# Sparse attention feeding a gated MLP: k, q and x turned by large DMA transposes, batch 1 turned by TensorE, rows loaded ahead, a new order of work

## The chip, the cores and the metric

The kernel runs on one core of one Trainium2 chip. The metric is the device time of one execution in microseconds (us). The profile is one further execution, taken by the hardware profiler; its times are counted from the start of its span. A run of the kernel before takes 227.52 us (median of 3, 227.52 to 228.05).

## What is computed

There are 4 batches of 8 heads, 768 positions and 64 numbers per head. Each query sees its own neighbourhood (fewer than 16 positions away) and 24 block keys, the maxima of k over blocks of 32 positions; the block values are the means of v. The attention output of all heads, 3072 rows of 512 numbers, then goes through an MLP with 2048 hidden units.

```python
k_sum = k.reshape(B, H, nb, block, D).max(axis=3)
v_sum = v.reshape(B, H, nb, block, D).mean(axis=3)
scores_l = scale * np.matmul(q, k.transpose(0, 1, 3, 2))
...
scores_s = scores_s + np.log(block)
scores_l_m = np.where(mask_l, scores_l, -1000000000.0)
scores_all = np.concatenate([scores_l_m, scores_s], axis=-1)
...
a = a / (np.sum(a, axis=-1, keepdims=True) + 1e-09)
v_all = np.concatenate([v, v_sum], axis=2)
return np.matmul(a, v_all).astype(np.float32)
```

```python
h = x @ w_in
relu6 = np.clip(h + 3.0, 0.0, 6.0)
g = h * relu6 / 6.0
return (g @ w_out).astype(np.float32)
```

## The kernel before

All matmuls are bf16. The attention of a batch works on four pairs of heads. The queries are cut into 12 blocks of 64, each with a window of 96 keys, and 24 block keys stand behind them, so that one score matmul has 120 rows of keys. For that, k and q must lie turned: the 64 numbers of a head on the partitions, the positions along the row. ScalarE takes the exponential out of PSUM (line 566), VectorE multiplies with the band mask (line 570), and TensorE multiplies with the values (line 671), which carry a column of ones so that the sum comes with them. VectorE divides (lines 705 and 709), TensorE turns the result (line 724), and a copy puts it into `x` (the helper in line 463).

The MLP works on eight tiles of 384 rows, two for each batch, numbered s = 0 to 7. One first-layer step has four matmuls of 384 columns (line 742), a ScalarE relu (line 747) and a VectorE multiplication (line 749), and there are 16 such steps for a tile. The second layer has 12 groups of four matmuls of 512 columns for a tile (line 762), a copy out and a store that SyncE (SP) issues (line 774).

Batch 0 has its own beginning: k and q are loaded in runs of rows and turned by TensorE (lines 479 and 522), half of the queries first, so that the MLP can begin early. Batches 1 to 3 load k and q in a raw form of 32 partitions (line 403: each load has 3072 pieces of 32 numbers), VectorE turns them in blocks of 32 x 32 (lines 623 and 627), and small copies by ScalarE or VectorE fill the overlap of the key windows. The means of v come from a matmul (lines 588 and 605). For batch 1 the values' overlap is copied on the chip; for batches 2 and 3 SP moves the overlap (lines 437 and 439) and the means (line 578) by DMA from SBUF to SBUF. Loads that change f32 to bf16 are issued by GpSimd (POOL), one after the other, through one queue.

Nothing is scheduled by hand within the loops: every operation is recorded with a name, and the string `ORDER` lists all names. `F21.3` is the fourth operation of the first layer of tile 2, in the second quarter of its hidden units; `G02` is the second layer of tile 0, rows 2; `s`, `v`, `u`, `h`, `w` are scores, values, means, overlap of v, and turning of k and q; `K`, `Q`, `V`, `I`, `O` are loads of k, q, v, w_in and w_out. A letter behind a colon chooses ScalarE or VectorE. `Plan.run` walks through the list, gives out buffers and PSUM banks, and sorts by its planned begin. Each engine then executes its own operations strictly in that order, so that a late operation holds up everything behind it on its engine. Of the 8 PSUM banks, 3 are for the first layer (`h`), 1 for the second (`o`), and 2 pairs for attention (`S`). Matmuls on a constant tile (`idle`, line 848) fill TensorE's planned gaps in the first 22 us.

Of the kernel before, what the change touches and what calls it, by code (L numbers as in the profile page):

```python
# [29 lines left out]
e.1 c.0 K00.0 c.8 z3.0 z1.0 z2.0 K01.0 c.1 Q000.0 K02.0 k00.0 c.2 Q010.0 c.3 c.4 e.0 k00.1 e.3 k00.2:D k00.4 V00.0 V01.0  # L30
k01.0 k01.2:A Q01w2.0 c.6 V02.0 V03.0 q010.0 q000.0 k01.1 k01.4 z0.0 q000.1:A q010.1:A k00.3:A Q01w1.0 I0.0 Q01w0.0 k01.3:A
k03.0 s000.0 k02.0 q030.0 k03.2:A q030.1:D e.2 c.7 I1.0 O0.0 I2.0 q020.0 s010.0 s000.1 s010.1 u00.0 q020.1:A s010.2 k03.1
k02.1 k03.4 k02.4 u00.1:A u00.2:D h010.0:D s000.2 u01.0 s030.0 s030.1 h011.0:D u01.1:D h000.0:D u01.2:D k02.2:A s020.0
s020.1 u02.0 h030.0:D u02.1:D s030.2 h020.0:A s020.2 u03.0 u03.1:D v01.0 v00.0 v00.2 v00.3 v01.2 v01.3 v02.1 I3.0 O2.0 O1.0
v00.1 v01.1 v02.4 v00.4 v00.5 h031.0:A h001.0:A k03.3:A u02.2:A v02.0 v00.6 v00.7:A v01.4 v02.2 v02.3 v01.5 q011.0 v01.6
v02.5 k02.3:A v01.7:D F00.0 v02.6 F00.5 F00.6 q001.0 v02.7:A F00.1 F00.2 q001.1:A F00.3 F00.7 c.5 h021.0:D q031.0 q011.1:A
F00.8 u01.3:D u00.3:D F00.4 F00.9 F01.0 q021.0 F01.3 F01.1 F01.2 q031.1:D F00.15 F00.10 s001.0 q021.1:A F01.4 F01.5 u03.2:D
F00.16 F00.17 s001.1 s001.2 s011.0 F00.11 F00.12 F00.13 F00.14 F01.9 F01.10 c.9 F01.11 F01.6 s011.1 F01.7 s011.2 F01.8
s021.0 F02.9 F02.10 F02.11 s021.1 s021.2 G02.0 s031.0 F02.0 F03.0 F03.3 s031.1 s031.2 F02.1 F03.1 F02.2 F03.2 v04.0 v03.0
v03.1 F03.4 v03.2 F03.5 v04.1 v04.2 F02.3 F02.6 F02.4 F02.5 v03.3 v03.4:A F03.9 v05.0 G02.1 v04.3 z0.1:P z3.1:P K11.0 K12.0  # L40
O3.0 K13.0 z1.1:P K10.0 V12.0 V10.0 V13.0 F03.10 F02.7 v05.1 v05.2 v05.3 v05.4:A F02.8 v04.4:D F03.11 F03.6 F03.7 F10.0
F03.8 F10.3 F10.1 F10.6 F10.4 F10.2 F10.5 F10.9 F10.7 F11.0 F10.8 F10.10 F11.3 F10.11 F11.1 F11.6 F11.2 F11.4 F11.5 F11.7
F11.8 F11.9 F12.6 Q10.0 V11.0 z2.1:P Q12.0 Q13.0 Q11.0 F11.10 F12.7 F11.11 F12.8 F13.0 F12.9 F13.1 F12.10 w12.0 w13.0 F13.2
h121.0:A w11.0 w13.3 w10.0 h100.0:D h130.0:D w10.3 G02.2 F13.6 F13.7 h111.0:D G02.3 F12.0 G02.4:A G01.0 G01.1 G01.2 G01.3
u1.0 h120.0:A F12.1 h101.0:A w10.2:A w13.4:A h131.0:A G01.4:A u1.1:A w12.2:A u1.6:A u1.2:A F12.11 w11.3 F13.8 u1.4:D w11.4:D
w12.3 w10.4:D w12.4:D V22.0 Q20.0 K22.0 K21.0 K20.0 K23.0 Q21.0 Q23.0 Q22.0 V23.0 V21.0 V20.0 w10.1 w10.5:D G00.0 G00.1
F13.9 G00.2 F12.3 G00.3 F13.10 u1.8:A w11.2:A F12.4 h110.0:A w11.1 F12.5 w11.5:D u1.9:D w13.1 w12.1 w12.5:D s100.0 s100.3
s100.1 G00.4:A s110.0 G00.5 s110.1 s110.3 F13.3 G12.0 s120.0 w13.2:A s120.3 s120.1 s110.2 w13.5:D F12.2 F13.11 s110.4 s100.2
F13.4 F13.5 s120.2 G12.1 G12.2 s130.0 s130.1 s130.3 s130.2 s120.4 G12.3 G12.4:A u1.5:A u1.3:A u1.7:A v10.0 G01.5 G12.5 v10.5
v10.1 v10.6 v10.2 s130.4 G11.0 G11.1 v12.0 v10.3 v12.1 v12.2 s100.4 w20.0 w20.3 G11.2 v10.4:A v10.7 v10.8:A v12.3 G11.3  # L50
v15.0 v15.1 v15.2 v12.4:A F20.0 G11.4:A F20.1 F20.3 F20.4 F20.6 v13.0 F20.7 F20.2 F20.5 F20.8 F21.0 F22.0 w20.2:A F21.1
F22.1 F20.9 v13.1 v13.2 w20.1 F20.10 w20.5:A G10.0 v13.3 F22.2 v13.4:A w20.4:A G10.1 F21.3 v15.3 v13.5 v13.6 F21.2 F20.11
F21.6 F22.6 v13.7 G10.2 G10.3 w21.1 w21.0 F21.4 v15.4:A F21.7 F22.7 v13.8:A s200.0 F21.5 F22.8 w21.2:A s200.3 F22.3 F22.4
F22.9 F22.10 w21.5:A u2.0 F21.8 w21.3 w21.4:D F22.5 F23.0 Q31.0 Q30.0 V30.0 V32.0 V31.0 V33.0 Q32.0 K33.0 Q33.0 K30.0 K32.0
K31.0 G10.4:A s200.1 u2.1:A F21.9 F21.10 F23.1 F22.11 G11.5 G02.5 u2.2 u2.3 G10.5 H2.0 u2.5 u2.4 w22.1 w22.0 F21.11 F23.3
F23.4 s210.0 G20.0 s210.3 s210.1 F23.2 F23.5 F30.0 G20.1 F23.9 F23.6 w22.5:D F30.1 w22.3 F23.7 w22.4:A F30.2 F23.10 w22.2:D
F23.8 F30.3 G20.2 F30.9 F30.10 s220.0 s220.1 F30.4 s200.2 F23.11 w23.1 F30.11 G20.3 F32.6 F32.0 G20.4:A w23.0 F32.1 w23.5:D
F32.2 F30.5 w23.2:A u3.0 w23.3 s210.2 s220.2 w30.1 G22.0 s220.3 F30.6 G22.1 u3.1:A F32.7 F32.8 w23.4:A F30.7 F30.8 s210.4
s220.4 G22.2 G22.3 G22.4:A s230.0 F31.6 s230.1 s230.3 s230.2 s230.4 F31.3 F31.0 G21.0 F31.4 F31.5 F31.1 v20.0 G21.1 F31.9
F31.10 v20.5 F31.2 v20.1 v20.6 s200.4 F31.11 G21.2 F33.6 F33.7 v20.2 F33.8 F31.7 F31.8 G21.3 F32.9 v20.3 F33.3 G21.4:A  # L60
v20.4:A F33.4 F32.10 u3.4 H2.1 H3.0 G22.5 G20.5 G21.5 v22.0 v25.0 F33.0 w30.0 v22.1 v22.2 F32.11 v25.1 v25.2 F33.1 F33.5
G32.0 F32.3 v20.7 v22.3 F32.4 G32.1 v20.8:A v22.4:A F33.9 F33.2 F32.5 w31.0 F33.10 w30.3 F33.11 F40.0 v23.0 G32.2 F40.9
F40.1 F40.3 w30.4:A F40.10 F40.4 v23.1 F40.2 v23.2 F40.5 F41.3 v23.3 G32.3 v23.4:A F41.4 G32.4:A F40.11 v23.5 F41.5 F40.6
F42.9 G30.0 G30.1 F42.3 v23.6 v23.7 G30.2 w33.0 F42.10 F42.11 w30.5:D w30.2:A F40.7 w31.3 F40.8 w31.2:A F42.4 F42.5 w31.1
F41.0 v25.3 F41.9 F41.1 F41.10 F41.2 F41.11 F42.0 F42.1 w32.1 F42.2 w31.5:D G30.3 F43.6 F43.9 v25.4:A G30.4:A v23.8:D w32.0
w32.3 w33.2:D G31.0 G31.1 w32.4:D F43.7 F43.10 F43.8 w31.4:A s310.0 s310.1 s310.3 G31.2 F43.3 F43.4 w32.5:A F43.5 G31.3
G31.4:A F50.0 F50.1 F42.6 F42.7 F43.11 w32.2:D w33.1 s300.0 s300.3 s300.1 H3.1 G31.5 G32.5 u3.5 u3.3 u3.2 G30.5 F41.6 G41.0
F41.7 F42.8 F50.2 s310.2 F41.8 F50.6 s320.0 F43.0 F50.7 w33.3 w33.5:A F43.1 s320.1 s320.3 F50.8 F43.2 s310.4 w33.4:D s300.2
F52.6 G41.1 F52.7 G41.2 F50.9 F50.10 F50.11 F52.8 F50.3 F50.4 F50.5 s330.0 s330.1 G41.3 G41.4:D s330.2 F52.3 F51.9 F52.0
G42.0 G42.1 F51.10 s330.3 s300.4 s320.2 F52.4 F52.1 F52.5 v30.0 G42.2 G42.3 F53.3 v30.1 v30.5 v30.2 F52.2 F51.11 F51.0  # L70
G42.4:A F51.6 F51.1 s330.4 s320.4 v30.3 G40.0 G40.1 F53.4 v30.4:A v30.6 F51.7 F51.8 F51.2 v35.0 v32.0 v32.1 F53.5 v35.1
v35.2 F52.9 G40.2 F51.3 F53.9 F52.10 F51.4 G40.3 G40.4:A F53.10 F52.11 G41.5 G42.5 G40.5 F51.5 v30.7 F53.6 F53.0 v32.2 v32.3
v32.4:A v30.8:D F53.7 F53.1 G50.0 G50.1 F53.8 F53.2 F53.11 G50.2 F60.3 F60.0 v33.0 F61.9 G50.3 F60.4 F60.1 F60.2 F61.10
F61.11 F60.5 G50.4:A F61.6 F61.0 F61.7 F61.1 v33.5 F61.8 F61.2 v33.1 v33.2 F62.9 F62.10 F62.11 G52.0 G52.1 G52.2 F62.6 G52.3
F62.3 G52.4:D F60.9 v33.3 G51.0 F62.4 F62.7 v33.4:A F62.5 F60.10 F60.11 F62.8 v33.6 G51.1 G51.2 F61.3 F61.4 F61.5 v35.3
F60.6 v35.4:A F63.3 v33.7 F60.7 F63.4 v33.8:A F63.9 F60.8 F63.5 F63.10 F63.11 G51.3 G51.4:A F62.0 F63.6 F62.1 F63.7 F62.2
F63.8 G50.5 G52.5 F70.0 F70.1 G62.0 F70.2 F73.3 F73.4 F73.5 F71.0 F71.1 F71.2 G62.1 F73.9 F63.0 F63.1 F63.2 F70.6 G62.2
G62.3 F70.7 F73.10 F73.11 F71.3 F72.6 F72.7 F71.4 F70.8 G62.4:D F71.5 F70.9 G60.0 F72.8 F70.10 G60.1 F72.0 F72.1 F72.2 G60.2
F71.9 F71.10 F70.11 F71.11 F71.6 G60.3 G60.4:A F70.3 F72.9 F70.4 F70.5 F72.10 F71.7 F72.11 F71.8 G61.0 G61.1 F73.0 F73.1
F73.2 G62.5 G51.5 G61.2 G72.0 F72.3 F72.4 G61.3 F72.5 G61.4:A F73.6 G70.0 G72.1 G72.2 F73.7 F73.8 G71.0 G71.2 G71.4 G71.6  # L80
G72.3 G72.4:D G61.5 G60.5 G72.5 G70.1 G71.7:A G71.8 G70.2 G71.1 G70.3 G70.4:D G70.5 G71.3 G71.5 G71.9 G71.10:A G71.11
"""

BANKS = ("S", "h", "o")


SLOW = 4.5
TURN = 0.11
LATER = 19.0
KRAW = 1.6  # L90
LAT = {"PE": 0.16, "ACT": 0.08, "DVE": 0.07, "POOL": 0.15}


# [8 lines left out]
class Op:  # L102
    def __init__(self, eng, cost, fn, prio, lat, alloc):
        self.eng, self.cost, self.fn, self.prio, self.lat, self.alloc = eng, cost, fn, prio, lat, alloc
        self.deps, self.bufs, self.end, self.begin, self.dma, self.els = set(), [], None, None, 0.0, 0
        self.alloc = [] if alloc is None else alloc if isinstance(alloc, list) else [alloc]


class Plan:
# [45 lines left out]
    def run(self):  # L155
# [7 lines left out]
        for token in ORDER.split():  # L163
# [6 lines left out]
            for d in o.deps:  # L170
                t = max(t, d.end if d.eng == e and not d.dma else d.end + d.lat)
# [47 lines left out]
def kernel(  # L219
# [568 lines left out]
    for c in range(3):  # L788
        load_w(c, -40 + c)
# [105 lines left out]
```

## Time and profile before

| what | value |
|---|---|
| median of the runs | 227.52 us |
| span of the profiled execution | 226.5 us |
| TensorE busy | 96% of the span, 2167 matmuls |
| VectorE, ScalarE, GpSimd busy | 70%, 59%, 29% |
| time on line 742 (first layer) | 95.4 us, 536 matmuls |
| time on line 762 (second layer) | 94.4 us, 400 matmuls |
| VectorE turning k and q (lines 623, 627) | 23.0 us, 24 instructions of about 0.96 us |
| DMA moved | 21.71 MB in 123066 packets, 114209 of them under 512 B |

Busy times of TensorE overlap a little, because matmuls are pipelined: four first-layer matmuls show 0.81 us of busy time but follow each other every 0.65 us. Starts are therefore the better measure. In the chain of waits each piece has its start, its length, its engine and its line.

### The profile page before, as it was taken

The numbers are of one execution on the slowest core, as the hardware profiler recorded it, in microseconds if no ns is written. First come the engines' busy times: TensorE is split into PE (matmuls) and PEld (weight loads), VectorE is DVE, ScalarE is ACT, GpSimd is POOL, SyncE is SP. The second block draws the span as 40 slices with busy tenths as digits, with TensorE's granted clock in tenths as the row PEclk, the third lists the DMA queues.
The fourth block names the chain that finished last, engine by engine and source line by source line (L and its number), as shares of the span: only waits on it lengthen the run. The fifth ranks groups of instructions, "written<-read, shape, count | busy, mean of one in ns | idle before, by whom it ended". The sixth has DMA issues, their size and how long they took to land.

```text
span 226.5 us, 5318 instructions
## 1 busy us (share of the span) xinstructions
PE 216.4 (96%) x2167; PEld 120.8 (53%) x2167; DVE 158.1 (70%) x329; ACT 132.9 (59%) x274; POOL 65.3 (29%) x75
## 2 busy tenths in 40 slices
PE   6799999999959999999999999999999999999992
PEld 2356765554534565555556555555555555555461
DVE  6667899889797999777789688777654556443211
ACT  2567797679886876858546567873444347435200
POOL 7997871645567648520000000000000000000000
PEclk9999999999997999999999999999999999999999
DMA  5999999999999999999271000331110110020222
GB/s 76 170 150 194 205 206 161 144 127 112 111 108 175 161 190 152 122 115 132 45 174 48 0 3 0 109 72 46 52 46 3 46 46 0 3 93 0 92 72 72
DMA packets 123066, 21.71 MB, mean 96 GB/s; under 512 B 114209, under 2 KB 120097, under 8 KB 123041
## 3 DMA queue, kind: packets, MB, share of 16 engines
q0 software_dynamic: 107920, 13.64, 138.4%
q1 hardware_dynamic: 15120, 7.73, 12.8%
q8 instruction: 17, 0.28, 0.5%
q14 instruction: 9, 0.07, 0.1%
HBM read 27.26 MB, written 6.29 MB: 148 GB/s over the span
## 4 chain that ended last, share of the span: by engine, by line
PE 68%; DMA 12%; POOL 11%; issue 5%; DVE 2%; ACT 1%; POOLq 0%
PE h L742 28%; PE o L762 28%; DMA wout<-in_moe_w_out_dram 7%; DMA qraw<-in_q_dram 5%; PE h L762 5%; POOL vaug L414 3%; PE S L671 3%; PE S L557 2%; PE S L724 2%; POOL qraw L403 2%; POOL win L448 1%; POOL qwide L394 1%; POOL first L374 1%; PE S L605 1%; DVE qT L627 1%
## 5 line engine op out<-in xcount | busy, mean ns | idle before, releaser
L749 DVE SCALAR_TENSOR_TENSOR g<-r,h 128x384 bf16<-128x384 f32 x128 | 67.8, 547 | 40.3 <-ACT r L747 38.6
L742 PE MATMUL h<-x,win 128*128 128x384 bf16 (+1 forms) x536 | 95.4, 319 | 0.2
L747 ACT ACTIVATE r<-h 128x384 f32<-128x384 f32 x128 | 61.4, 491 | 51.0 <-PE h L742 48.9
L762 PE MATMUL o<-wout,g 128*128 128x512 bf16 x336 | 83.7, 384 | 0.0
L742 PEld LDWEIGHTS <-win 128*128 128x128 bf16 x536 | 49.6, 98 | 35.5 <-issue 0.8
L762 PEld LDWEIGHTS <-g 128*128 128x128 bf16 x400 | 37.9, 98 | 36.1 <-issue 1.3
L566 ACT ACTIVATE at<-S 120x768 bf16<-120x768 f32 x32 | 24.9, 813 | 6.2 <-PE S L557 6.2
L414 POOL DMA_DIRECT2D vaug<-in_v_dram x16 | 15.0, 941 | 11.1 <-issue 5.5
L709 DVE TENSOR_TENSOR xn<-S,rc 128x512 bf16<-128x512 f32 (+1 forms) x25 | 16.0, 642 | 0.5
L570 DVE TENSOR_TENSOR at<-at,mask 96x768 bf16<-96x768 bf16 x28 | 14.8, 548 | 1.2 <-ACT at L566 0.9
L463 ACT COPY ot<-o 128x512 f32<-128x512 f32 x18 | 10.6, 588 | 8.4 <-PE o L762 8.4
L463 ACT COPY x<-S 128x512 bf16<-128x512 bf16 x18 | 10.3, 585 | 3.9 <-PE S L724 2.8
L403 POOL DMA_DIRECT2D qraw<-in_q_dram x8 | 10.5, 1313 | 7.3 <-issue 5.2
L557 PEld LDWEIGHTS <-kaug 64*128 64x128 bf16 x384 | 7.3, 97 | 9.1 <-issue 6.4
L403 POOL DMA_DIRECT2D kraw<-in_k_dram x8 | 10.5, 1318 | 4.6 <-issue 2.9
L557 PE MATMUL S<-qT,kaug 64*128 64x64 bf16 x384 | 9.6, 194 | 2.3 <-ACT at L566 0.9
L640 DVE TENSOR_REDUCE red<-kaug 128x24 bf16<-128x768 bf16 x12 | 11.3, 941 | 0.1
L762 PE MATMUL h<-wout,g 128*128 128x512 bf16 (+1 forms) x64 | 10.7, 326 | 0.0
L671 PEld LDWEIGHTS <-at 120*64 120x64 bf16 x360 | 7.0, 111 | 5.2 <-issue 4.5
L848 PE MATMUL o<-idle 128*128 128x512 bf16 x20 | 7.7, 472 | 1.6 <-DVE idle L300 1.6
L671 PE MATMUL S<-vaug,at 120*64 120x65 bf16 x352 | 8.4, 197 | 0.1
L724 PEld LDWEIGHTS <-xn 128*128 128x128 bf16 x96 | 6.9, 98 | 2.8
(100 smaller groups left out, 165.3 us busy)
## 6 DMA issues: line engine op xcount, KB each, us to landing
out_dram<-ot SPq DMA_DIRECT2D x19, 256.0 KB
vaug<-in_v_dram POOLq DMA_DIRECT2D x16, 192.0 KB, 9.1
win<-in_moe_w_in_dram POOLq DMA_DIRECT2D x4, 512.0 KB, 11.0
wout<-in_moe_w_out_dram POOLq DMA_DIRECT2D x4, 512.0 KB, 16.4
kraw<-in_k_dram POOLq DMA_DIRECT2D x8, 192.0 KB, 14.8
qraw<-in_q_dram POOLq DMA_DIRECT2D x8, 192.0 KB, 10.7
first<-in_k_dram POOLq DMA_DIRECT2D x6, 192.0 KB, 8.3
first<-in_q_dram POOLq DMA_DIRECT2D x6, 192.0 KB, 9.6
```

What stands on the lines that cost most here:

```text
L403: op("POOL", 1.32, lambda src=src, o=o, hs=hs, ds=ds, rows=rows: nc.gpsimd.dma_start(out=o[rows], in_=src[b, hs].rearrange("h (c r) d -> r ...
L414: op("POOL", 0.95, lambda: nc.gpsimd.dma_start(out=o[BLK:WIN, lo:hi, 0:D], in_=rows[:, lo:hi]), w=[("v", b % 2, c)], prio=prio, dma=1.25, ...
L463: {"ACT": nc.scalar.copy, "DVE": nc.vector.tensor_copy, "POOL": nc.gpsimd.tensor_copy}[eng](o, i)
L557: nc.tensor.matmul(X[p, half].slot[:, j, i * QB:(i + 1) * QB], kaug[p][rows, t], qT[rows, p, t * QB:(t + 1) * QB], start=not masked, stop= ...
L566: op("ACT", act(2 * HALF), lambda a=a, x=x: nc.scalar.activation(a, x.slot[0:KEYS, :, 0:HALF], AF.Exp, scale=scl), r=[x], w=[("at", p, hal ...
L570: op("DVE", 0.57, lambda m=m, half=half: nc.vector.tensor_tensor(m, m, mask[:, low(half):low(half) + HQ].unsqueeze(1).to_broadcast([WIN, 2 ...
L671: nc.tensor.matmul(y, a[:, cols], vaug[b % 2][0:KEYS, h, t, 0:D + 1], start=True, stop=True)
L709: nc.vector.tensor_tensor(o, src[..., 0:D], r.unsqueeze(len(r.shape)).to_broadcast(list(o.shape)), op=ALU.mult)
L742: nc.tensor.matmul(h.slot[:, lo * 128:hi * 128], w_in_sb[:, kt, ft * 128:(ft + 1) * 128], xt[s].slot[:, kt, lo * 128:hi * 128], start=(kt ...
L747: op("ACT", act(HALF), lambda: nc.scalar.activation(r.slot[:], h.slot[:, 0:HALF], AF.Relu, bias=0.5, scale=1.0 / 6.0), r=[h], w=[r], prio= ...
L749: op("DVE", dve(HALF), lambda: nc.vector.scalar_tensor_tensor(gt[s].slot[:, ft], r.slot[:], 1.0, h.slot[:, 0:HALF], op0=ALU.min, op1=ALU.m ...
L762: nc.tensor.matmul(o.slot[:, a:z], gt[s].slot[:, ft, ts * 128:(ts + 1) * 128], w_out_sb[:, ft, a:z], start=(ft == 0), stop=(ft == NFT - 1))
```

## The change

- K and q of batches 1 to 3 are loaded in natural rows (`load_nat`, 12 loads a batch, each 128 positions of all heads in pieces of 64 numbers) into two buffers `nat`, and the turned forms lie in two buffers each (`kb`, `qb`), so that the rows of a batch can be loaded while the batch before is in use.
- For batches 2 and 3, SP issues four DMA transposes a batch (`k_turn`, `q_turn`), and one for each 128 rows of `x` (the new branch in `finish`). For batch 1, TensorE turns k and q (`turn_pe`, 48 transposes of 128 columns), and ScalarE or VectorE copies them out.
- The overlap and the block maxima of k are made for all pairs at once (`turn`). The overlap of v is loaded from DRAM by POOL for all three batches (`load_halo`), and the means are copied on the chip for all of them.
- The zeros in front of v's first block are needed for batch 0 alone, and ScalarE may write them (`empty`).
- `values` takes the six row groups of a batch two by two; `ORDER` and the numbers that the planner works with are new; the planner puts 15 filler matmuls where it put 35.

The first loads stand in `ORDER` as follows (other names left out; what POOL makes itself is in brackets):

```diff
-K00.0 K01.0 (ident) Q000.0 K02.0 (band) Q010.0 V00.0 V01.0 Q01w2.0 (ind) V02.0 V03.0 Q01w1.0 I0.0 Q01w0.0 I1.0 O0.0 I2.0 I3.0 O1.0 O2.0
+K01.0 Q010.0 K02.0 (band) K00.0 (ident) Q000.0 V01.0 V00.0 V02.0 V03.0 (ind) Q01w2.0 Q01w1.0 Q01w0.0 I0.0 I1.0 I3.0 I2.0 (12 loads of K1 and Q1) O0.0 O1.0 O2.0 O3.0 h11.0 h10.0 V10.0
```

```diff
+    def load_nat(b, name, u):
...
+            nc.gpsimd.dma_start(out=o[n:128], in_=src[b, :, lo + n:lo + 128].rearrange("h r d -> r h d"))
...
+    def load_halo(b):
...
+            op("POOL", 0.945, lambda lo=lo, hi=hi: nc.gpsimd.dma_start(out=o[0:BLK, lo + 1:hi, 0:D], in_=rows[QB - BLK:QB, lo:hi - 1]),
...
+    def q_turn(b, x):
...
+            nc.sync.dma_start(out=qb[i][:, NP * lo:NP * (lo + n)], in_=nat[i]["Q"][:, lo:lo + n].rearrange("p u m -> p (u m)"), transpose=True)
...
+    def k_turn(b, e):
...
+            nc.sync.dma_start(out=kb[i][:, n * e:n * e + n, BLK:WIN], in_=nat[i]["K"][64 * e:64 * e + 64].rearrange("p u m -> p (u m)"),
+                              transpose=True)
...
+    def turn_pe(p):
...
+                for u in range(NS):
+                    nc.tensor.transpose(bank(T).bitcast(BF16)[:, u * 128:(u + 1) * 128], nat[1][name][:, u, p * 128:(p + 1) * 128], ident[:])
...
+        def third(eng, e):
...
+        def most(e):
+            nc.vector.tensor_reduce(red.slot[:].rearrange("x (p u e n) -> x e u p n", p=NP, u=NS, e=2)[:, e],
+                                    w[:, n * e:n * e + n, BLK:WIN].rearrange("x (u p) (n c) -> x u p n c", p=NP, n=2), axis=AX.X, op=ALU.max)
...
+        if b > 1:
+            op("SP", 1.3, lambda: nc.sync.dma_start(out=xt[s].slot[:, :, cols], in_=xn.slot[:], transpose=True),
+               r=[xn] + done, dma=0.6, kind="turn", **new)
+            return
...
-        values(b, (0, 1), base + 17)
-        values(b, (2,), base + 21)
-        values(b, (3, 4), base + 25)
-        values(b, (5,), base + 31)
+        for Ts in ((0, 1), (2, 3), (4, 5)):
+            values(b, Ts)
...
+                nc.scalar.mul(o, idle[0:BLK, 0:D].bitcast(F32).unsqueeze(1).unsqueeze(1).to_broadcast([BLK, 2, NQ, D // 2]), 0.0)
```

In the built program TensorE has 40 fewer entries (20 fillers with their weight loads); the 48 transposes of `x` that go are replaced by the 48 of batch 1. VectorE loses its 24 block transposes. SP issues 20 DMA transposes and 29 stores, and no other copy. In SP's order the transposes of batch 2 are `k2e0`, a store, `q2x1`, two stores, `q2x0`, `k2e1`.

## The prediction

> **What bounds the kernel now.** I read the page's table of engines, then TensorE (PE) in stretches of 5 us, then the chain of waits, then SP's timeline.
>
> ```profile
> PE 216.4 (96%) x2167; PEld 120.8 (53%) x2167; DVE 158.1 (70%) x329; ACT 132.9 (59%) x274; POOL 65.3 (29%) x75
> ...
> 60.00:65.00 5.00, 3.57 (x40) 1.92 (x38) 4.68 (x10) 4.11 (x8) 3.46 (x4) 1.00 6.11 107
> 65.00:70.00 5.00, 4.13 (x57) 2.15 (x57) 4.90 (x11) 3.88 (x8) 3.59 (x4) 0.72 6.04 121
> 70.00:75.00 5.00, 4.86 (x71) 2.41 (x70) 3.21 (x9) 4.29 (x7) 3.97 (x4) 0.94 2.66 174
> ...
> 105.00:110.00 5.00, 5.00 (x47) 2.47 (x47) 5.00 (x10) 3.06 (x9) 0.00 (x0) 1.00 0.45 52
> ```
>
> The first pair in a stretch is its length and PE's busy time; the last three numbers are granted clock, DMA share and GB/s. PE is the bound, and full but for the beginning and 55 to 75 us. The chain says what it waited for there, and gives the price of each group of matmuls:
>
> ```profile
> 52.18 10.43 DMA qraw<-in_q_dram
> 62.64 0.99 DVE qT L627
> ...
> 97.14 0.86 PE o L762 x4
> 98.00 1.95 PE h L742 x12
> ...
> 101.46 0.46 PE S L557 x24
> 101.92 0.97 PE o L762 x4
> ...
> 104.19 0.78 PE S L605 x48
> ...
> 112.56 0.63 PE S L671 x32
> ...
> 117.83 0.22 PE S L724 x4
> ...
> 222.51 0.37 ACT ot L463
> ```
>
> Batch 1's q lands at 62.6 and VectorE (DVE) then turns it, 0.97 us a pair. To see what is lost, I sum PE's order from its first L742, at 25.43 in PE's timeline, by these rows: 500 wide L742 x 0.1625 and 36 narrow x 0.055 (83.2), L762 at 0.216, half that for 256 columns (82.9), 97 transposes x 0.055 (5.3), 336 score matmuls x 0.0192 (6.4), 336 value x 0.0197 (6.6), 144 means x 0.0165 (2.4), 2 fillers (0.4), and 29 changes to narrow matmuls x 0.1 (the 0.97 beside 0.86). That is 190.2. The last matmul ends at 222.5, so 197.1 went by and **6.8 us are lost**. At the means of batch 1 (57.2) the trace is 1.6 behind the sum, at those of batch 2 (92.2) 6.5, at the end 6.8: five of them lie in that one place.
>
> **The sum.** The time is: first L742, plus PE's work behind it, plus losses, plus the tail.
>
> *Work behind it.* The same sum over the new order: 48 transposes of x go and 48 of k and q come; batch 0's rest moves ahead (90 transposes, 324 score matmuls, no filler), 28 changes. 189.1, so 1.1 less.
>
> *First L742.* Before, the last exponential of batch 0's first half decides:
>
> ```profile
> 20.05 0.79 ACT L566 ACTIVATE at<-S 120x768 bf16<-120x768 f32 x1
> ```
>
> It ends at 20.84, and L742 follows 4.6 later. The new first loads are the same five; the last, issued at 5.6 before, took 6.3 to land (11.9), and as the bytes are the same I keep that. Its transposes take 0.5; then ScalarE (ACT) has, in its order, q 0.48, two k copies 0.64 each, exp 0.81, cast 0.26, q 0.48, overlap 0.71 + 0.29, exp 0.81, cast 0.26, exp 0.81 twice: 7.0, ending at 19.4. With the same 4.6, L742 starts at **24.0**. Zeros written by ACT (3 of 0.7 to 0.83) lie in its idle time before its first copy (4.5 idle before 6.6) and take 2.1 off DVE; they cost nothing, at most those 2.5 if ACT is wanted early. The bounds of 24.0: no gain, 25.4; and 22.4, when w_in's first quarter is there, 7.3 after its issue (its least landing) at 15.1 by POOL's order.
>
> *Loads up to batch 1's means.* Before, w_in's first quarter lands at 21.1 (13.8 + 7.3), and w_out's third at 35.3, five quarters and a q piece later: 2.67 a quarter. In the new order one more q piece lies ahead: quarters at 22.0, 24.7, 27.3, 30.0. Then K1 and Q1, 1.57 MB as written, in pieces of 64 numbers; from 8 to 16 us such loads of v and q run at 154 GB/s, so 10.2: 40.1. w_out follows at 42.8, 45.4, 48.1, 50.8, v and its overlap (1.17 MB, 7.6) at 58.5. By the sum PE wants k at 37.7 (there at 36), q at 42.9, w_out at 45.5 to 51.9, the means at 60.2. Cover is 1.1 to 2.8, and beyond it lateness costs PE one for one. The 5 us of batch 1 go, with DVE's turns off its path; the new copies out (0.6 to 0.8 each) and the chain means, cast, copies, values are as tight as the stage before 50 us that lost 1.0. I book **1.0** (0 to 3).
>
> *k and q of batches 2 and 3.* K2's last load lies 2.29 MB behind: 14.7, so 73.2. Then SP, one queue, issues four transposes of 0.39 MB, with three stores between (1.3). ACT's `w2.4` and DVE's `w2.0` wait for the first at 81.1, `w2.1` for the last at 86.7. Both engines wait in order, so behind them stand relus and multiplications of tiles 2 and 3; with 3 PSUM banks PE stops about two steps later. The four may take 86.7 - 73.2 - 1.3 = 12.2, or 3.0 each. No row shows a transpose by DMA. Nearest rows, SP's timeline:
>
> ```profile
> 112.82 0.64 SPq L437 DMA_DIRECT2D vaug<-vaug  x1
> 113.55 4.61 SPq L774 DMA_DIRECT2D out_dram<-ot  x3
> 118.40 0.61 SPq L439 DMA_DIRECT2D vaug<-vaug  x1
> ```
>
> A copy of 0.39 MB inside SBUF in 128-byte pieces holds up three stores, 1.1 alone, to 4.6, and about 5.5 passes until the queue is free. At the rate of weight loads (205 GB/s) it would be 1.9. A transpose reads long rows, as a store does, and writes short ones, as that copy does: nearer to neither, so I take the middle of 1.9 each and of 5.5 for k (128-byte columns) and half of it for q (256): 12.2 in all, just inside. Loss **0** (0 to 10, if all four are like the copy). Batch 3's loads end 3.14 MB later (20.4), near 94, and `w3.0` comes at 110: more room.
> By the Trainium skill (Advanced Engine Details and Errata, X-Bar Transpose (TRN2)) these run as fast as plain DMAs, 350 to 400 GB/s; an estimate from that is 1.0 each and no loss, where the copy's row gives 10.
>
> *x of batches 2 and 3.* PE's 0.22 a group is already out of the sum. What is added is a wait: tile 4's last rows leave the values at 110.5, DVE needs 0.2 + 0.2 + 0.68 + 0.68 and its latency (112.4); a transpose of 0.13 MB takes a store's issue and landing at least (0.38 + about 2, from the end of the trace), at most 4.3 with the copy's rate; PE wants it at 115.4. Late by -0.6 to 1.3; tile 6 (142.9 to 149.4) has 2 more room. I book **1.0** with what else is tight (0 to 3).
>
> Tail: 4.0, last matmul to the end of the span, same last steps. Span: 24.0 + 189.1 + 2.0 + 4.0 = 219.1. The profiled execution had 226.5 against a median of 227.5, so **220.1**.
>
> **The rivals.**
>
> *SP holds the transposes up (slower).* Place: `k2e0` to `k2e1`. If each takes 5.5 like the copy, `w2.1` is 10 late: 230. It decides from 4.9 each (12.2 + 7.4 = 19.6 for four): from there the gain is gone. For it: the row above, and batch 3's loads fill the queues at the same time. Against: pieces there are 3040 of 128 B, while a store of 2 KB rows costs 0.38.
> Against the change speaks the Trainium skill (DMA: Bandwidth & Descriptors, the part "Why a DMA increments its semaphore by 16 and not by 1"): before the newer chip's fast path, a transpose inside SBUF cost the issuing sequencer 262,144 cycles for 8,192 tiles, the transfer not counted. No run here shows it.
>
> *The clock in the beginning.* With 15 fillers instead of 35, PE idles more before its first L742. Two stretches show the price:
>
> ```profile
> 63.00:66.40 3.40, 1.23 (x48) 1.05 (x47) 3.30 (x7) 2.57 (x4) 2.74 (x3) 1.00 6.40 106
> 67.40:70.40 3.00, 3.00 (x30) 1.25 (x29) 2.96 (x8) 1.88 (x4) 1.92 (x3) 0.50 5.11 144
> ```
>
> At 36% busy the clock fell to half. Between 18 and 24 us PE has 3.2 of work (9 value groups, 18 transposes); at half the clock it takes 3.2 more: 223.3. Against: the score and means groups keep 13 to 18 us nearly full.
>
> *Loads at the raw rate.* If rows come at the 109 GB/s of 56 to 66 us, K1 and Q1 take 4.2 more and K2 with Q2 some 4.7 more; 2.4 and 6.4 exceed the cover: 228.9. Against: those were 128-byte reads, the new ones are 256, as in 8 to 16 us.
>
> *It doesn't do what it says*: the beginning gains nothing and only the five go: 221.5; inside the forecast.
>
> **How the numbers follow.** Forecast 0.62, with its own range 216.5 to 223; clock 0.12 (222 to 226); loads 0.08 (224 to 229, half of it below 226.8); transposes 0.18 (227 and more). A difference of 0.3% (0.7 us) is about what can be told from none here. Faster: 0.62 + 0.12 + 0.03 = 0.77; same 0.04, from the edges of loads and transposes; slower 0.19. The range 216.5 to 228.5 leaves out the bulk of the transposes' case and a little below.
>
> **What would show it.** Right: first L742 near 24; PE full from 57 to 75, clock 1.00 there; SP's issues of the k and q transposes under 3 us and `w2.0` not waiting for DMA more than 1; last matmul near 215. Wrong: DVE or ACT waiting for `kb` by DMA for several us near 80 to 90, PE waiting for `nat` or `wout`, or a granted clock below 1 before 26 us.

## The result, and the profile after

The changed kernel takes **234.44 us** (median of 4, 233.06 to 235.09) against 227.79 us for the kernel before in the same session: a ratio of 1.0265, 95% interval 1.0213 to 1.0317. It is slower; the forecast was 220.1, between 216.5 and 228.5. Ratios leave disturbed executions out, so they can differ a little from the quotient of two medians.

First the page of the changed kernel: the table of engines, TensorE's granted clock in 40 slices, and the group of the block maxima.

```profile
PE 211.0 (90%) x2123; PEld 120.9 (52%) x2147; DVE 141.1 (60%) x293; ACT 124.0 (53%) x238; POOL 71.9 (31%) x95
...
PEclk9979799999999999958999999999999999999999
...
L676 DVE TENSOR_REDUCE red<-kb 128x48 bf16<-128x1536 bf16 x6 | 10.5, 1747 | 7.2 <-DMA kb<-nat 7.2
```

PE has 5.4 us less to do and is busy for 90% of the span instead of 96%: the time went into gaps, and the clock row shows three places at less than full clock. PE in stretches of 5 us (length, PE's busy time, weight loads, the other engines; at the end clock, DMA share, GB/s):

```profile
10.00:15.00 5.00, 3.87 (x68) 2.70 (x69) 2.72 (x5) 1.03 (x4) 4.86 (x9) 0.66 2.22 160
...
20.00:25.00 5.00, 3.45 (x89) 2.76 (x87) 4.71 (x13) 4.30 (x11) 3.89 (x7) 1.00 1.25 207
...
60.00:65.00 5.00, 4.84 (x85) 2.50 (x88) 2.81 (x6) 3.91 (x7) 5.00 (x6) 1.00 2.27 147
65.00:70.00 5.00, 4.39 (x91) 2.48 (x79) 4.79 (x11) 4.03 (x7) 5.00 (x8) 1.00 2.39 151
...
95.00:100.00 5.00, 0.18 (x1) 0.00 (x0) 0.37 (x1) 0.00 (x0) 1.04 (x2) 1.00 1.75 186
100.00:105.00 5.00, 3.11 (x32) 1.53 (x32) 3.71 (x7) 2.35 (x3) 5.00 (x7) 0.51 2.39 152
```

The hole of the kernel before at 60 to 70 us is gone (4.84 and 4.39 us of PE's work where 3.57 and 4.13 stood). A new one stands at 95 to 102, with half the clock behind it. The chain of waits (start, length, what) says what ended it, and PE's timeline how long it was:

```profile
83.99 2.11 SPq L556
...
86.14 13.46 DMA kb<-nat
...
99.70 1.60 issue
101.30 0.56 DVE g L791
```

```profile
93.29 1.89 PE L804 MATMUL o<-wout,g 128*128 128x512 bf16 x8
101.89 1.44 PE L784 MATMUL h<-x,win 128*128 128x384 bf16 x4 [6.72 <-DVE g L791]
```

SP's timeline at that place: line 565 are the k transposes, 556 those of q, 815 and 816 are stores; the second number is the issue.

```profile
76.84 1.57 SPq L565 DMA_TRANSPOSE kb<-nat  x1
...
80.11 1.95 SPq L556 DMA_TRANSPOSE qb<-nat  x1
...
83.99 2.11 SPq L556 DMA_TRANSPOSE qb<-nat  x1
86.14 7.32 SPq L565 DMA_TRANSPOSE kb<-nat  x1
```

The second k transpose of batch 2 (`k2e1`) lands 13.46 us after its issue began, at 99.6; line 565's answer gives 5.1, 5.1 and 13.5 us from issue to landing as least, median and most. DVE stands at `w2.1`, the second half of the block maxima, for 7.2 us, and the multiplications of the MLP stand behind it in DVE's order, so PE stops 6.7 us. When it goes on, the clock is 0.51 from 101.8 to 107.0, and 5.1 us of busy time there are worth 2.6 less. Together 9.3 us.

The sum of the forecast against this profile: the first L784 (old L742) at 27.48 instead of 24.0, 3.5; from there to the last matmul's end (228.99) 201.5 instead of 191.1, 10.4, of which the stop is 9.3; the tail 4.4 instead of 4.0. That is 14.3, the 233.4 against 219.1.

### The profile page after: what moved, and what is told of

Read it like the earlier page. It is cut to its first block, busy times and chain, and to the rows that moved or that the text cites. A ratio compares the mean times of both kernels' runs of the same rounds, so it can differ in the third digit from the quotient of the medians.

```text
span 233.4 us, 5207 instructions
## 1 busy us (share of the span) xinstructions
PE 211.0 (90%) x2123; PEld 120.9 (52%) x2147; DVE 141.1 (60%) x293; ACT 124.0 (53%) x238; POOL 71.9 (31%) x95
## 4 chain that ended last, share of the span: by engine, by line
PE 72%; DMA 13%; DVE 6%; SPq 3%; issue 3%; ACT 2%; POOL 1%; ACTq 0%; DVEq 0%; POOLq 0%
PE h L784 32%; PE o L804 25%; DMA kb<-nat 6%; DMA nat<-in_k_dram 3%; PE h L804 3%; DVE vaug L480 3%; PE S L711 3%; PE S L610 2%; DMA x<-xn 2%; DVE g L791 2%; SPq L815 1%; PE S L578 1%; PE S L651 1%; DMA out_dram<-ot 1%; SPq L556 1%
## 5 line engine op out<-in xcount | busy, mean ns | idle before, releaser
L784 PE MATMUL h<-x,win 128*128 128x384 bf16 (+1 forms) x536 | 97.2, 325 | 8.1 <-DVE g L791 7.0
L804 PE MATMUL o<-wout,g 128*128 128x512 bf16 x313 | 78.7, 379 | 1.5 <-issue 0.5
L784 PEld LDWEIGHTS <-win 128*128 128x128 bf16 x536 | 50.1, 99 | 43.2 <-issue 9.3
L420 POOL DMA_DIRECT2D nat<-in_k_dram x18 | 16.7, 966 | 4.7 <-DMA win<-in_moe_w_in_dram 4.6
L420 POOL DMA_DIRECT2D nat<-in_q_dram x18 | 16.5, 930 | 0.9 <-DMA win<-in_moe_w_in_dram 0.9
L748 DVE TENSOR_TENSOR xn<-S,rc 128x512 bf16<-128x512 f32 x23 | 15.3, 683 | 0.1
L676 DVE TENSOR_REDUCE red<-kb 128x48 bf16<-128x1536 bf16 x6 | 10.5, 1747 | 7.2 <-DMA kb<-nat 7.2
L804 PE MATMUL h<-wout,g 128*128 128x256 bf16 (+1 forms) x63 | 11.0, 325 | 0.1
L610 PEld LDWEIGHTS <-kb 64*128 64x128 bf16 x384 | 7.0, 98 | 6.6 <-issue 5.3
L610 PE MATMUL S<-qb,kb 64*128 64x64 bf16 x384 | 9.4, 195 | 0.0
L480 ACT COPY vaug<-vs 24x768 bf16<-24x768 bf16 x10 | 8.3, 828 | 0.2
L480 ACT COPY kb<-h 128x480 bf16<-128x480 bf16 (+3 forms) x15 | 4.8, 395 | 6.3 <-DVE red L516 6.3
## 6 DMA issues: line engine op xcount, KB each, us to landing
vaug<-in_v_dram POOLq DMA_DIRECT2D x16, 192.0 KB, 10.8
```

Of the source, the lines that this page charges most:

```text
L420: nc.gpsimd.dma_start(out=o[n:128], in_=src[b, :, lo + n:lo + 128].rearrange("h r d -> r h d"))
L480: {"ACT": nc.scalar.copy, "DVE": nc.vector.tensor_copy, "POOL": nc.gpsimd.tensor_copy}[eng](o, i)
L610: nc.tensor.matmul(X[p, half].slot[:, j, i * QB:(i + 1) * QB], keys, asks, start=not masked, stop=not masked or i == HQ - 1)
L748: nc.vector.tensor_tensor(o, src[..., 0:D], r.unsqueeze(len(r.shape)).to_broadcast(list(o.shape)), op=ALU.mult)
L784: nc.tensor.matmul(h.slot[:, lo * 128:hi * 128], w_in_sb[:, kt, ft * 128:(ft + 1) * 128], xt[s].slot[:, kt, lo * 128:hi * 128], start=(kt ...
L804: nc.tensor.matmul(o.slot[:, a:z], gt[s].slot[:, ft, ts * 128:(ts + 1) * 128], w_out_sb[:, ft, a:z], start=(ft == 0), stop=(ft == NFT - 1))
```

## The experiments

All ratios are to the kernel before, run beside each.

| run | what | median us | ratio, 95% interval | span |
|---|---|---|---|---|
| hold | (the changed kernel again) | 233.43 | 1.0276 (1.0213 to 1.0339) | 232.6 |
| kfirst | both k transposes first | 234.23 | 1.0289 (1.0213 to 1.0366) | 232.3 |
| fill | 14 more fillers | 234.09 | 1.0314 (1.0244 to 1.0384) | 232.3 |
| fillk | kfirst + fill | 229.86 | 1.0134 (1.0056 to 1.0212) | 227.8 |
| gate | value loads of batch 3 held | 236.89 | 1.0412 (1.0351 to 1.0473) | 235.4 |
| pe2 | batch 2 by TensorE | 227.90 | 0.9963 (0.9912 to 1.0014) | 223.6 |
| pe2f | pe2 + fillers | 227.74 | 1.0008 (0.9967 to 1.0050) | 225.0 |
| gatek | gate + k first + fillers | 231.22 | 1.0148 (1.0073 to 1.0223) | 227.6 |
| gate3 | gate, other order of loads | 235.40 | 1.0295 (1.0227 to 1.0362) | 235.3 |
| fill2 | fillers up to the landing | 234.20 | 1.0241 (1.0188 to 1.0293) | 234.4 |
| bnf | before, 8 fillers fewer | 228.39 | 0.9995 (0.9962 to 1.0028) | 226.3 |
| kq | batch 2: k by DMA, q by TensorE | 225.10 | 0.9861 (0.9817 to 0.9905) | 222.8 |
| kq2 | kq again | 224.74 | 0.9900 (0.9852 to 0.9948) | 224.6 |
| kqs | kq, store between the transposes | 224.29 | 0.9879 (0.9831 to 0.9927) | 222.7 |
| kqn | kq without more fillers | 227.25 | 0.9988 (0.9951 to 1.0026) | 226.7 |
| kqx | kq, x by TensorE | 232.06 | 1.0212 (1.0160 to 1.0265) | 230.0 |
| kqload | kq, eight loads more | 236.72 | 1.0384 (1.0301 to 1.0467) | 235.1 |

### Why the transpose landed late

**hold.**

```diff
+           r=[("kt", 0, 1, 0)] if (b, c) == (3, 1) else (), w=[("v", b % 2, c)], dma=1.28, els=1536)
```

> The changed kernel, but the first of batch 3's value loads on POOL's queue (V31, and with it everything behind it on that queue: the rest of batch 2's and 3's values, issued at 80.1 to 88.8 us before) waits until the second k transpose of batch 2 has landed. Theory A (the value loads and the transposes share the DMA engines, and the loads in flight made the second k transpose land 13.5 us after it was issued): its issue takes under 2.5 us instead of 7.3, it lands under 7 us after, the PE stop of 6.7 us at 95 and the half clock behind it (100 to 106.5) go, some 9 us; given back are up to 4 us at batch 3, whose values then start 8 to 10 us later. Span 226 to 229. Theory B (four large transposes issued one after the other on SP's queue hold each other up, whatever else is loaded): the issue is still 5 us or more, the landing 10 us or more, the stop stays; span 232 or more.

The dependence went into the planner's list alone; an engine waits only for what an instruction touches, and nothing was held: POOL issued those loads at 78.3 to 87.2 us, before `k2e1` landed at 99.6. So this run says nothing on either theory. It is the changed kernel once more, and shows the same kind of stop (8.6 us; issue 7.00 us, landing 12.9 after it began) and a first L784 at 25.91 instead of 27.48: the beginning varies from run to run.

**kfirst.** In `ORDER`: `k2e0.0 k2e1.0 G00.5 q2x1.0 G10.5 q2x0.0`.

> The changed kernel with one name moved in SP's order: both k transposes of batch 2 stand first, then the two q transposes; nothing else is changed. Theory A (contention with the value loads issued from 80.1 us on): the second k transpose is issued at 78.5, ahead of the loads, and lands by 86; the means of batch 2 (w2.1) are no longer late; the last q transpose takes over the slow place and lands at 93 to 100, about when the scores of batch 2 want it (97). The stop at 95 falls from 6.7 us to 0 to 3, and the half clock behind it goes with it: span 224 to 228. Theory C (DVE is late at w2.1 for a cause of its own, not because of the landing): the stop stays over 5 us, span 232 or more.

The block maxima no longer wait for `kb` (1.5 us of DVE's waits for it are left, at an overlap copy), and PE's longest wait becomes that for q:

```profile
PE S L610 <- DMA qb<-nat: 2.6, 1, 2.6
```

The last transpose of the four, now q's, lands 11.7 us after its issue at 87.2, again near 99; the wait moved to another instruction. Theory C falls. The time did not move outside the interval; smaller stops followed (output copies, sums, half the clock at 100 to 105).

**gate.** The real hold: POOL copies two columns that `k2e1` writes, then issues the loads.

```diff
+        op("POOL", 0.2, lambda: nc.gpsimd.tensor_copy(look[:], kb[0][:, NP * NS, BLK:BLK + 2]), r=[("kt", 0, 1, 0)], w=["look"])
...
-V31.0 h31.0 V23.0 V22.0 h30.0 V32.0 V33.0 h22.0 V30.0 u2.0 h32.0 F32.2 u3.0
+V23.0 V22.0 h22.0 y.0 V31.0 h31.0 h30.0 V32.0 V33.0 V30.0 u2.0 h32.0 F32.2
```

> The changed kernel, but the value loads of batch 3 (seven of the eleven that POOL issued between 80 and 89 us) stand behind a small POOL copy that reads what the second k transpose of batch 2 wrote; the other values of batch 2 go ahead of it, and the sums of batch 3 come some 8 us later in PE's order. SP's order is as in the changed kernel (second k transpose last of four). Theory A (loads in flight on the same DMA engines stretch the transposes): the second k transpose lands within 8 us of its issue at about 86, by 94; PE's stop before 102 falls under 1.5 us, no half clock behind it; span 224 to 228. Theory B (four transposes of 393 KB take some 5.7 us each, whatever is loaded beside them, and stand behind each other): it still lands 11 us or more after its issue, at 97 or later; the stop is 4 us or more, span 230 or more.

The timelines of SP and of POOL in this run:

```profile
88.96 3.86 SPq L566 DMA_TRANSPOSE kb<-nat  x1
```

```profile
94.33 0.18 POOL L689 COPY look<-kb 128x2 bf16<-128x2 bf16 x1 [16.17 <-DMA kb<-nat]
```

The loads held are seven of ten (nine had been issued by 89.2 in the changed kernel, not eleven). `k2e1` landed 5.2 us after its issue began, against 13.5, and PE is full from 78 to 102: theory A in its own numbers. The order of the landings says the same. The four transposes, in SP's order, took 5.1, 8.2, 11.3 and 13.5 us to land in the changed kernel; here, in the same order, 9.8, 9.5, 7.2 and 5.2. Theory B, by which they stand behind each other, would have them rise here too; they fall as the loads drain, which POOL issued earlier in this run. In the trace's view of the DMA queues from 80 to 84 us, the packets of POOL's queue took 92% of the 16 engines' time here and 3% in the changed kernel. The time is no argument, for it is worse: the held loads made batch 3's k late (PE waits 3.2 us at 118.3 for DVE, which waits for `kb`), and this profile's beginning ran at half the clock from 10 to 22, with the first layer at 30.5. **gatek** and **gate3** tried to make something of the hold:

> Held value loads of batch 3, both k transposes first on SP, and the fillers of the run before, together. Theory A: the four transposes of batch 2 have landed by 94, no PE stop over 1.5 us between 85 and 107; span 222 to 225.5, faster than the kernel before the change. Theory B: the last q transpose lands at 97 or later and PE waits for it 2 to 4 us, span 227 or more.

> Loads held until the second k transpose of batch 2 has landed, as in the run with the small POOL copy, but k and q of batch 3 then come ahead of its values, the k transposes stand first and third on SP with the stores between them, the sums of batch 3 are later still, and the fillers are those of the run before. Theory A: k2 lands by 87, no stop over 1.5 us from 85 to 107, no wait of 3 us for batch 3; span 222.5 to 226. If the held loads are needed sooner than they can come: stops of 3 us or more between 107 and 125, span 228 or more.

In gatek the stop for the block maxima is gone, but theory A's "no stop over 1.5" is missed: PE waits 2.4 us at 85 to 90 for an output buffer, whose store stands behind both transposes on SP (their issue took 7.5 us together), and the clock behind it is 0.66 at 90 to 95; with its first layer at 26.5 the span is 227.6. In gate3 PE waits 9.8 us for batch 3's values. Holding loads pays for one late thing with another.

**kqload.** The opposite: loads where there were none. It starts from kq (below); eight value loads of 192 KB into rows that nobody reads any more, behind batch 3's loads. The other engines' programs are the same.

```diff
+            op("POOL", 0.945, lambda i=i, rows=rows, to=to: nc.gpsimd.dma_start(out=to, in_=rows[:, 2 * NQ * (i % 4):2 * NQ * (i % 4) + 2 * NQ]), w=[("spare", i)], dma=1.28, els=1536)
```

> The run that turned only batch 2's q by TensorE, with eight more value loads of 192 KB (read again into rows that nobody reads any more) on POOL's queue right behind the loads of batch 3, issued at about 101 to 108 us; every other engine's program is the same. Theory A (loads in flight stretch a large transpose): batch 3's transposes, issued at 104 to 112, land 7 us or more after their issue instead of 3.8 to 5.2, or are longer in issue. Theory B (a transpose's time is its own and that of the one ahead of it): they land in 3.8 to 5.5 us as before. The time says less, for the scores of batch 3 come late: 225 to 229.

DMA issues around batch 3's transposes (count, KB, median us from issue to landing), first in kq, then in kqload:

```profile
qb<-nat SPq DMA_TRANSPOSE x2, 3.8
kb<-nat SPq DMA_TRANSPOSE x2, 5.2
```

```profile
nat<-in_v_dram POOLq DMA_DIRECT2D x8, 192.0 KB, 10.5
...
kb<-nat SPq DMA_TRANSPOSE x2, 12.2
qb<-nat SPq DMA_TRANSPOSE x1, 11.0
```

And PE's timeline in kqload:

```profile
122.77 1.44 PE L795 MATMUL h<-x,win 128*128 128x384 bf16 x4 [4.07 <-DVE g L802]
```

From 3.8 and 5.2 to 11.0 and 12.2, with 4.5 us of waiting for `kb` on DVE and the same kind of stop as in the changed kernel, one batch later. The packets of POOL's queue took 155% of the 16 engines' time from 106 to 121 us, against 11% in kq from 103 to 118. Nothing but the loads differs, so loads in flight do it. The time, 236.7, lies outside the 225 to 229 expected; PE also waits 4.2 us once for an output copy.

### What each part is worth

**pe2, pe2f.** Batch 2 turned by TensorE, as batch 1.

```diff
-        if b == 1:
+        if b < 3:
             for p in range(NP):
-                turn_pe(p)
+                turn_pe(b, p)
```

> The changed kernel, but k and q of batch 2 are turned by TensorE (8 groups of 6 turns, and 8 copies out by ACT and DVE, as in batch 1); batch 3 and x stay with the transposes. If the late landing of batch 2's transposes is the cause of the stop at 95 (6.7 us and some 2.6 at half clock): both go, 8 x 0.34 = 2.7 us of turns come back; span 225.5 to 228. If the value loads or DVE's order were late in themselves: PE stops 4 us or more between 85 and 107 all the same, span 230 or more.

> As the run before (batch 2 turned by TensorE), with more filler matmuls in the beginning: 14 instead of 5 ahead of the turns that wait for the last of the first five loads, and the old rule after that. If PE's idle stretch ahead of that landing brings the half clock: no granted clock under 0.95 up to 30 us, first L784 at 24.8 to 25.8; span 224 to 226.5. If the fillers buy nothing: first L784 at 26 or later, span as the run before.

The stop and the half clock behind it are gone: PE has 9.65 of the 10 us from 85 to 95 and 9.79 of the next ten. The time is that of the kernel before: the change's whole loss hung on the four transposes of one batch. The fillers changed nothing measurable in the time here.

**kq.** K of batch 2 by two DMA transposes, ahead of the stores; q by TensorE (four groups, four copies on ACT); 14 fillers ahead of the turns that wait for the third of the first five loads (the expectations of fill2 call it the last).

```diff
-k2e0.0 G00.5 q2x1.0 G10.5 q2x0.0 k2e1.0 F23.6 F23.7 G12.2 G12.3 w2.4:A F23.5 F21.8 F23.8 w2.0
+k2e0.0 k2e1.0 G00.5 G10.5 F23.6 F23.7 G12.2 G12.3 w2.4:A F23.5 q20.0 F21.8 F23.8 q20.1:A w2.0
```

> The changed kernel with the fillers of the run before, and of batch 2 only k by transposes (both, one behind the other, ahead of the stores); its q is turned by TensorE (4 groups of 6 turns, 1.4 us, and 4 copies on ACT). Half as many bytes go through the transposes beside the value loads. Theory A: both k transposes land by 88, w2.1 isn't late, no stop over 1.5 us between 85 and 107 and no half clock; span 222.5 to 225.5, time 224 to 227, at or under the kernel before. If even two transposes beside the loads are late: stop of 3 us or more, time 229 or more.

PE in two stretches of 12 us of this run:

```profile
84.00:96.00 12.00, 11.95 (x83) 7.02 (x82) 8.92 (x14) 9.73 (x18) 6.35 (x9) 1.00 2.14 189
96.00:108.00 12.00, 11.79 (x223) 6.86 (x224) 8.54 (x18) 8.86 (x18) 4.93 (x6) 1.00 1.71 140
```

PE is full, and the version beats both kernels: 225.10, and 224.74 when run again, 1.4% and 1.0% under the kernel before.

> The same program as the version that measured 225.1 (0.986 of the kernel before), a second time. If that was the program: 224.5 to 226.5 and a ratio of 0.982 to 0.993; if it was the chip or a lucky profile: ratio 0.995 or more.

**kqn, kqs.** kqn is kq with the changed kernel's fillers; kqs puts one store between the two transposes.

> The run that turned only batch 2's q by TensorE, without its additional filler matmuls: beginning as in the changed kernel. If fillers buy nothing on the median (as the two runs with batch 2 wholly on TensorE said, 227.7 with and 227.9 without): 225.1 within 1, under the kernel before by 0.8 to 1.6%. If they are worth what the half clock costs in the changed kernel's profile: 227 or more.

In kqn's profile the first layer starts at 24.5, 2.5 earlier than in kq, and it loses that again at 85 to 95: ACT waits for a store, PE behind it for 3.2 us, and the clock then falls to 0.50 at 90 to 95:

```profile
88.97 0.59 ACT L480 COPY ot<-o 128x512 f32<-128x512 f32 x1 [3.60 <-DMA out_dram<-ot]
```

> The version with only batch 2's q turned by TensorE and the additional fillers; on SP the output store that stood behind both k transposes of batch 2 now stands between them, nothing else differs on any engine. Theory (SP's order is a price of its own: the store waits behind a transpose's issue, and ACT for the buffer): no wait of ACT for a store over 0.5 us from 80 to 95, PE's wait for L480's copy gone; time 224 to 226, at or under the same version's second run. Rival (the second k transpose, 2 us later, makes the means of batch 2 late): a stop for w2.1 of 2 us or more, time 227 or more.

In kqs no wait of PE for an output copy is left (1.1 in kq2, 3.2 in kqn), and the medians, 224.29 beside 224.74 on the same chip, don't tell the two apart. What separates kqn from kq is not settled: fillers gained nothing between pe2 and pe2f, and kqn's store wait, with the half clock behind it, is in one profile only.

**kqx.** X of batches 2 and 3 by TensorE again, on kq.

```diff
-        if b > 1:
+        if b > 3:
             op("SP", 1.3, lambda: nc.sync.dma_start(out=xt[s].slot[:, :, cols], in_=xn.slot[:], transpose=True),
```

> The run that turned only batch 2's q by TensorE (with its fillers), and x of batches 2 and 3 turned by TensorE too: 12 groups of 4 turns (2.7 us by the forecast's row) and 12 copies on ACT in place of 12 transposes on SP. Theory (x by transposes gains PE time and costs about one wait of 1.0 us): 1.5 to 2.7 us slower than 225.1, 226.6 to 227.8. Rival (the copies and turns fill gaps anyway, the wait for x was worth as much): 225.1 within 0.7.

7 us slower than kq by the medians (7.8 in the profiles, from the first layer to the last matmul), more than either side expected. 2.7 are the turns. Part of the rest is my order: each turn stands where the transpose was issued, right behind the division, and PE waits for it, 3.1 us in four places, once for long:

```profile
164.14 0.40 PE L770 MATMUL S<-ident,xn 128*128 128x128 bf16 x4 [1.83 <-DVE xn L752]
```

Another 1.1 is a wait for an output copy; what makes up the remaining microsecond is not shown. So of the 7 us the turns alone are shown to be the price of x by TensorE; 7 us is no measure of it.

### The beginning

**fill, fillk, fill2.**

```diff
+            n += 6 * (o.key == "k03.0")
```

(fill2; fill has the old rule without this line, fillk is fill with both k transposes first.)

> The changed kernel with the old rule for the filler matmuls of the beginning: 14 more of them, 3 ahead of the turns at 10.8 us and the others one by one in the gaps of the first 23 us. Theory (PE's idle stretches, 3.2 us ahead of 10.8 and some 3 us between 20 and 25, brought the half clock at 10.8 to 15 and 25 to 28.7): no granted clock under 0.9 up to 30 us, first matmul of the first layer (L784) at 25.0 to 26.0 instead of 27.5, span shorter by 1.5 to 2.5: 231 to 232. Rival (the beginning is set by the ACT and DVE work of batch 0, PE waits for it anyway): first L784 at 27 or later, span 233 or more.

> The two edits before together (both k transposes first, 14 more filler matmuls). If both theories hold, their gains add up: span 222 to 226, and the kernel is faster than the one before the change (span 226.5). If the fillers only shift the wait or the q transpose takes over the whole stop: span 228 or more.

> The changed kernel with 14 instead of 5 filler matmuls ahead of the turns that wait for the last of the first five loads, and the old rule after that; everything else as in the changed kernel. Theory: PE's wait there falls from 3.2 us to 1 or less, no granted clock under 0.95 before 90 us, first L784 at 25.2 to 26.5 instead of 27.5; the stop at 95 stays (5 us or more, half clock after it); time 231 to 233. Rival (the start costs nothing): time 234.4 as the changed kernel.

The load that PE's turns wait for near 10.8 us in these runs is the third of the first five, not the last. In fill the wait was still 2.3 us and the clock fell all the same. In fill2 the wait was 0.5, the clock stayed at 1.00 until 95, and the first L784 came at 26.62; the time is that of the changed kernel, 234.2. fillk is 4.4 us under kfirst, though neither part alone gained: in its profile the first layer starts at 25.7 and no granted clock falls, while kfirst's had half the clock at 24 to 28 and at 100 to 106. The extra fillers have a price of their own. Between pe2 and pe2f, which differ in them alone, the time from the last first load's landing to the last exponential's end goes from 7.6 to 8.6 us; in fillk and fill2 it is 8.6 too.

**bnf.** The kernel before without the seven fillers at 7.96 us and one more.

> The kernel before the change, with 8 of its filler matmuls left out: the 7 that it runs at 7.96 us, ahead of the turns that wait for the last of the first five loads (10.9 us), and one more. Nothing else differs. Theory (PE idle for some 2.5 us or more right ahead of that landing gives half clock afterwards, with or without the change): PE waits some 3 us there instead of 1.3, the granted clock is near 0.5 for 4 us or more before 30 us, the first L742 comes 1 to 3 us later than 25.4; median ratio 1.005 to 1.015. Rival (the half clock of the changed kernel has another cause): clock 1.0 throughout the beginning, time as before within 0.3%.

The k load that PE waits for there came at about 9 us in this profile, the wait was 1.1 instead of the 3 foreseen, the clock stayed at 1.00 up to 65 us, and the time is the same. The theory's condition didn't occur, so the run neither bears it out nor refutes it; the rival's outcome stands.

## Why the prediction was wrong

**The step that failed: "I take the middle ... 12.2 in all, just inside. Loss 0."** It was the rival "SP holds the transposes up", at its place (`k2e0` to `k2e1`) and of about its size (230 foreseen, chance 0.18). The forecast priced a transpose by a copy and a store that ran where little else was loaded (the rows near 105 to 115 us of the kernel before move 52 to 58 GB/s), and took one price for all four. The runs show two: 3.8 to 5.2 us from issue to landing with little else loaded, in batch 3 of kq, and up to 14.0 (fill) with value loads in flight. What four in a row would take with nothing beside them no run shows; an estimate, from three issues of 1.4 to 2.1 and a landing some 5 us after the last begins, is 9 to 11 us, within the budget of 12.2. Beside POOL's loads they took 22.8, stores included (76.8 to 99.6), and the 6.7 us of stop with 2.6 at half clock stand where the forecast has 0. POOL issued nine of those loads from 80.1 to 89.2 us, between the first transpose and the landing of the last. The sentence "batch 3's loads fill the queues at the same time" stood in the rival, without a price of its own. From 88 to 99 us in the changed kernel the packets of POOL's queue took 117% of the 16 engines' time and those of SP's 63%, at 158 GB/s together.

The Trainium skill (DMA: Bandwidth & Descriptors, section "SWDGE vs HWDGE vs iDMA") says that each DMA engine takes turns between the internal queues that the two kinds of issuers feed. The runs fit this: a transpose lands later with loads in flight (11.0 and 12.2 us in kqload) than without (3.8 and 5.2 in kq). The Trainium skill's rate for transposes (Advanced Engine Details and Errata, section X-Bar Transpose (TRN2)), by which I had estimated 1.0 us each, is not met here: 0.39 MB took 3.7 us at the least, the issue included (pe2). The Trainium skill's cost of a transpose's issue in cycles (DMA: Bandwidth & Descriptors, section "Why a DMA increments its semaphore by 16 and not by 1"), held against the change in the forecast, is not told apart by any run: an issue took 1.4 to 2.1 us with little else loaded.

**First L742 at 24.0: a term mis-sized by 3.5.** The last of the five loads (q, issued at 5.6) landed at 13.1 instead of 11.9, which is 1.2. From there to the last exponential's end (21.55) 8.4 us passed instead of 7.5. ACT's timeline shows where that 0.9 lies, in a copy that waits for PE's turns of this q:

```profile
14.73 0.48 ACT L480 COPY qb<-o 128x384 bf16<-128x384 bf16 x1 [1.58 <-PE o L534]
```

The copy begins 1.6 us after the landing where the forecast had 0.5, with PE at less than full clock (0.66 from 10 to 15); ACT's own work behind it took 6.8, the forecast 7.0. From the exponential to the first L784 it was 5.9 instead of 4.6, the last 1.3, part of it at a reduced clock again (0.75 at 24 to 26). The other profiles tell the two terms apart. In kfirst, hold, pe2 and kqn the exponential ended 7.4 to 7.6 after the landing: that sum was right. The first layer followed the exponential by 5.1 us or more in every profile of the new order, and by 5.3 to 5.6 where the clock held (fillk, fill2, pe2f): the 4.6 copied from the kernel before was too small, by 0.7 or more even at full clock; why is open.

From the last landing to the first layer it is 13.5 in the kernel before, 13.0 in kfirst, pe2 and kqn, 13.6 in hold, 14.4 in the changed kernel and 17.7 in gate, with the half clock in a different place in each. So the new beginning was worth 0.2 to 0.9 us where it went well (first layer at 24.5 to 25.2 against 25.43), not 1.4, and a late load or half the clock took it away.

**The clock in the beginning** (rival, 0.12) came true in part, in other places than foreseen: 0.66 at 10 to 15 and half at 25 to 28.8, while at 20 to 25, in the stretch that the rival named, it was 1.00. Fillers and clock go together: without extra fillers it fell in all six profiles of this beginning (after, hold, kfirst, pe2, gate, kqn); with them it held in eight (fillk, fill2, pe2f, gatek, gate3, kqs, kqx, kqload) and fell in three (fill, kq, kq2). That they are its cause is not shown, and their own microsecond takes the gain back.

**Right:** the loads and batch 1. PE had 17.28 of the 20 us from 55 to 75 before and 19.12 after, the granted clock there rose from 0.91 to 1.00, and PE waits nowhere for `nat` or `wout` there. So most of the 5 us did go: PE idles 0.9 there instead of 2.7. **X by DMA**, booked at 1.0: PE waits 1.1 in all for it. **Work behind the first layer**, 189.1: in kq, with 1.4 more, the last matmul ends at 219.6, 192.6 after the first L786; that bears the sum out with 2.1 lost, the losses booked (2.0).

## What to carry to other kernels

A transfer's price depends on what is in flight beside it: before moving work from an engine to DMA, list the loads in flight between its issue and the moment it is wanted, and price it beside them. If the instruction that waits for it stands in the middle of an in-order engine, one late transfer stops everything behind it, so move as little as must be there in time (here k alone, ahead of the stores) and leave the rest to an engine with known latency. Sum a start-up chain over all engines that hand over to each other, not over the busiest one's list.

## What the runs showed of the hardware

- A DMA transpose of 0.39 MB inside SBUF: issue 1.4 to 2.1 us, landing 3.7 to 5.3 us after the issue began with little else loaded (batch 3 of kq, pe2, gate); 9.5 to 14.0 with loads of POOL's queue in flight (gate, kqload, the changed kernel, fill). When transposes queue up beside loads, SP itself is held: 7.0 to 8.0 us for one issue (7.00 in hold, 7.32 in the changed kernel, 7.95 in fill), and the stores behind it. `k2e0` took 5.1 in the changed kernel, where POOL's queue moved little (3% of the engines' time at 80 to 84 us), and 9.8 in gate, where it moved much (92%).
- Half clock without a long idle stretch: in kq, where PE was not idle there for more than 0.7 us at a time, it was busy 1.43 and 1.33 us in two stretches of 2 us, and the clock fell to half at 15 to 19.6 us; in pe2f, with 1.36 and 1.33 at the same place, it did not.
- The landing of loads may be out of reach of a plan: the last of the first five loads landed between 11.5 and 13.1 us in the profiles of the new order, which issue it alike, and the third of them between 9.6 and 10.8.
